# A planned order for the first token block, and the low words' three bits on ScalarE

## The chip, the cores and the metric

The kernel runs on one core of one Trainium2 chip. The metric is the device time of one execution, in microseconds (us). Before the change three runs gave 1130.69, 1131.46 and 1132.25 us, so the median is 1131.46 us.

## The reference

Three stages follow each other. The first is a decayed linear attention: for each of 4 batches and 8 heads a 64 x 64 state is carried over 768 positions. The other two are dense layers on the 3072 x 512 result, each with a width of 2048 inside. All inputs have float32 or float64 values; the two layers' weights are float64.

```python
state = gamma * state + outer(k[t], v[t])          # attention, per batch and head
y[t]  = scale * (q[t] @ state)
h = x @ w_in;  g = h * sigmoid(1.702 * h);  x = g @ w_out          # layer 1
h = x @ w_in2; g = P(h) / (Q(h) + 1e-6);    out = g @ w_out2       # layer 2, P cubic, Q quadratic in |h|
```

## The kernel before

**Tiling.** The 3072 tokens are 24 chunks of 128 (six chunks per batch). Layer 1 works on six blocks of 512 tokens, four chunks each, so chunks 0 to 3 must be through the attention before the first block can start. A block has 16 steps j, one for each 128 of the 2048 inner columns. A step has two products on TensorE: `g1(j)` (12 matmuls of 128x512 into a PSUM bank `hp`) and, two steps later, `g2(j)` (12 matmuls of 128x512 that add into four banks `o`). Between them lie a sigmoid on ScalarE (L1044), a multiply on VectorE (L1045) and the split of the result into a high part `gh` (ScalarE, L1053) and a low part `gl` (VectorE, L1054). High and low parts are fp32r, and three products of them stand for one fp32 product. While block b runs, the attention of the chunks of block b+1 is slotted between its steps.

**The chunks.** A chunk is scaled (VectorE, L715 for chunks 0 to 3, then q on VectorE at L717 and k on ScalarE at L709), transposed (PE L738, copied by ScalarE L740), scored and summed (PE L777, L800), masked and added to the state (VectorE L785, L815), and multiplied out in two halves (PE L838). The first half needs one small copy (`xh`, ScalarE L889) before the second may start; then three more copies (L882) and four subtractions (`xl`, VectorE L884) follow.

**The weights.** Layer 1's weights are 32 pieces u of 128x512, taken in the order i0, i1, i2, o0, i3, o1, i4, o2, ... (i: a piece of `w_in`, for `g1`; o: of `w_out`, for `g2`). Each piece arrives as pairs of 32-bit words of float64 values and is turned into fp32 during the first block, as its steps need it:

- `w_first`: absolute value of the high words, times 2^16 (ScalarE L523);
- `w_bits`: clamp (VectorE L529), the top three bits of the low words as an integer 0 to 7 (VectorE L530), shift and or of both (VectorE L533);
- `w_sign`: the sign (VectorE L540). The first four o pieces are kept whole in the tiles `held` here, and `g2` uses them as plain fp32 (L956);
- `w_high`, `w_low`: fp32r high part (ScalarE L554) and the rest (VectorE L562).

The tiles of some pieces are reused for later ones, so the load of a later piece waits for `w_low` of an earlier one.

**What sets the order.** All four engines and the DMA queue of SyncE (SP) work strictly in the order written. The opening (chunks 0 to 3 and the first pieces) is written by hand in `opening()`; `keep_warm(n)` puts n matmuls on zeros there. After it `prep` takes one piece per half step in a software pipeline, the main loop calls `g1` two steps ahead of `g2`, and the chunks 4 to 7 come at fixed half steps. A scheduler in the framework then settles how these streams lie beside each other. Layer 2 has a planner of its own, which the change leaves alone.

Of the kernel before, what the change touches and what calls it, by code (L numbers as in the profile page):

```python
# [23 lines left out]
KD = DM // P  # L24
KF = DFF // P
EPS = 1e-6
MAXF = float(np.array(0x4FEFFFFF, np.uint32).view(np.float32))


# [411 lines left out]
def tile_kernel(ctx: ExitStack, tc: tile.TileContext, q, k, v, w1i, w1o, w2i, w2o, pa, pb, cst, out):  # L441
# [62 lines left out]
    def w_load(layer, u):  # L504
# [11 lines left out]
            nc.sync.dma_start(out=s.rearrange("p f t -> p (f t)"), in_=src.bitcast(I32)[fc * P : (fc + 1) * P, :])  # L516
        STG[u] = s

    def w_first(u):
        s = STG[u]  # L520
        m = io.tile([P, DM], F32, tag="u", name=f"u{u}")
        U[u] = m
        nc.scalar.activation(out=m, in_=s[:, :, 1].bitcast(F32), func=ACTF.Abs, scale=2.0**16)  # L523

    def w_bits(u):
        s, m = STG[u], U[u]
        mi = m.bitcast(I32)
        lo_word = s[:, :, 0]
        nc.vector.tensor_scalar(out=m, in0=m, scalar1=2.0, scalar2=MAXF, op0=ALU.max, op1=ALU.min)  # L529
        low = nc.vector.tensor_scalar(out=lo_word, in0=lo_word.bitcast(U32), scalar1=2.0**-29, scalar2=7.0, op0=ALU.mult, op1=ALU.min)  # L530
        if PIN:
            tc.keep_in_program_order(low)
        nc.vector.scalar_tensor_tensor(out=mi, in0=mi, scalar=3, in1=s[:, :, 0], op0=ALU.logical_shift_left, op1=ALU.bitwise_or)  # L533

    def w_sign(u, in_place=True):
        s, mi = STG[u], U.pop(u).bitcast(I32)
        r = s[:, :, 1] if in_place else mi
        if in_place and u in LATER:
            r = HELD[LATER.index(u)]
        nc.vector.scalar_tensor_tensor(out=r, in0=s[:, :, 1], scalar=-(2**31), in1=mi, op0=ALU.bitwise_and, op1=ALU.bitwise_or)  # L540
        STG[u] = r.bitcast(F32)

    def w_high(layer, u, whole=True):
        nm, fc = unit(layer, u)
        if whole and layer == 1 and u in LATER:
            return
        m = STG[u]
        shape = [P, KD, P] if nm == "i" else [P, DM]
        if nm == "i":
            m = m.rearrange("p (c f) -> p c f", c=KD)  # L550
        pair = wp.tile([P, 2, *shape[1:]], F32R, tag=f"w{u}", name=f"w{nm}{layer}_{fc}")
        STG[u] = m
        W[layer, nm, fc] = (pair[:, 0], pair[:, 1])
        high = nc.scalar.copy(out=pair[:, 0], in_=m)  # L554
        if not whole:
            tc.keep_in_program_order(high)

    def w_low(layer, u, whole=True):
        if whole and layer == 1 and u in LATER:
            return  # L560
        hi, lo = W[layer, *unit(layer, u)]
        low = nc.vector.tensor_tensor(out=lo, in0=STG.pop(u), in1=hi.bitcast(F32), op=ALU.subtract)  # L562
        if not whole:
            tc.keep_in_program_order(low)
# [128 lines left out]
    def load_chunk(c):  # L693
        for nm in "qkv":
            load_raw(c, nm)
# [47 lines left out]
    def att_T(c, tg, alt=None):  # L743
        for n, nm in enumerate("qk"):
            att_T1(c, nm, tg[n], alt)
# [73 lines left out]
    def att_S(c, tg, alt=None, sums=True):  # L819
        pss = [ps(tg[n], f"pS{n}_{c}").rearrange("a x t -> a (x t)") for n in range(2)]  # L820
        scores(c, pss, 0, 0)
        if sums:
            state_sums(c, pss, {(x, n) for x in range(2) for n in range(2)})
        masks(c, pss, 0, 0, alt)
        if sums:
            states_of(c, pss)

    def att_Y0(c, tg, xh, xl, o, joint=False):

# [39 lines left out]

        def bank(n, x):
            return py[n ^ x][:, 128 * x : 128 * x + 128].rearrange("a (k t) -> a k t", t=D)

        def rest():
            half(1)
# [21 lines left out]
    def att_Y1(c):  # L898
        REST.pop(c)()
# [209 lines left out]
        chunk += n  # L1109

    NU = 2 * KF
    prepped = [0]

    after_split = {}
    tenant = {}
# [9 lines left out]
        if t:  # L1125
            tenant[t] = u

    def prep(upto):

        while prepped[0] < min(upto, NU + 2):  # L1130
            s = prepped[0]
            if 2 <= s:
                w_high(1, s - 2)
            if s < NU:
                w_first(s)
            if 1 <= s <= NU:
                w_bits(s - 1)
            if 2 <= s:
                w_low(1, s - 2)
                for u in after_split.get(s - 2, ()):  # L1140
                    w_load(1, u)
            if 1 <= s <= NU:
                w_sign(s - 1)
            prepped[0] += 1

    E = mybir.EngineType
    with tc.manual_schedule(engines={E.SP}):
        nc.vector.memset(warm, 0.0)
# [5 lines left out]
            load_raw(1, nm)  # L1154
        for nm in "qk":
            load_raw(2, nm, ch, "z")
        w_load(1, 0)
        load_raw(2, "v", ch, "z")
        both = ws.tile([P, 2, H, D], F32, tag="s", name="raw3")
        load_raw(3, "q", at=both[:, 0])  # L1160
        load_raw(3, "k", at=both[:, 1])
        load_raw(3, "v", gp, "gl")
        for u in early[1:5]:
            w_load(1, u)
# [11 lines left out]
        for nm, t in (("q", "xh"), ("k", "xl")):  # L1176
            FIRST[nm] = x_pair(t, 1, F32, f"first_{nm}")

        def T(c):
            att_T(c, ("a", "a"), "gh" if c % 2 else None)  # L1180

        def S(c):
            att_S(c, ("o2", "o1") if c % 2 else ("o0", "o1"), "gl" if c % 2 else None)

        def Y(c):
            att_Y0(c, ("h", "h"), *X0, c * P)
            keep_warm(2)
            att_Y1(c)

        def opening():  # L1190
            keep_warm(10)
            scale_chunk(0)
            att_T1(0, "q", "a")
            keep_warm(2)
            att_T1(0, "k", "a")
            scale_chunk(1)
            keep_warm(2)
            S(0)
            att_T1(1, "q", "a", "gh")
            att_T1(1, "k", "a", "gh")  # L1200
            Y(0)
            load_chunk(4)
            S(1)
            scale_chunk(2)
            keep_warm(2)
            Y(1)
            for u in early[5:9]:
                w_load(1, u)
            load_chunk(5)
            for u in early[9:]:  # L1210
                w_load(1, u)
            T(2)
            w_first(0)
            scale_chunk(3)
            keep_warm(2)
            S(2)
            w_bits(0)
            w_sign(0)
            T(3)
            w_first(1)  # L1220
            w_high(1, 0)
            Y(2)
            S(3)
            w_low(1, 0)
            for u in after_split.get(0, ()):
                w_load(1, u)
            w_bits(1)
            keep_warm(4)
            Y(3)
            w_sign(1)  # L1230
            w_first(2)
            prepped[0] = 3
            prep(4)
            keep_warm(3)
            scale_chunk(4)

        with tc.manual_schedule(engines={E.PE, E.DVE, E.Activation, E.Pool}):
            opening()
        PIN.append(True)
        for x in range(2):  # L1240
            held = ws.tile([P, 2, DM], I32, tag="s", name=f"held{x}")
            HELD += [held[:, 0], held[:, 1]]
        nxt = 0
        conv0 = KF + 2
        XS0 = 4 * KF + KF - 2
        XB = []
# [27 lines left out]
                        if f:  # L1274
                            f()

        for i in range(-lead[1], NS):
            p0 = 2 * i + 6
            prep(p0)
            while nxt < NS and nxt - lead[steps[nxt][0]] <= i:  # L1280
                j = nxt
                nxt += 1
                g1(j)
                act1_a(j)
                prep(p0 + 1)
                act1_b(j)
            if i == -1:
                scale_chunk(5)
            if 0 <= i - KF + 2 < WHOLE:
                w_high(1, LATER[i - KF + 2], False)  # L1290
                w_low(1, LATER[i - KF + 2], False)
            if i == KF:
                tc.keep_in_program_order(nc.scalar.activation(out=ab[:, 6:7], in_=ab[:, 5:6], func=ACTF.Abs))
            if i < 0:
                continue
            for f in todo[i][0]:
                f()
            g2(i)
            layer, bi, fc, t0, n = steps[i]
            if fc == KF - 1 and bi < 5:  # L1300
                evac(bi)
            for f in todo[i][1]:
                f()

            if i >= XS0:
                x_piece(i)
            if i >= NS - 4:
                load_wo(2 * (i - NS + 4))
                load_wo(2 * (i - NS + 4) + 1)
# [46 lines left out]
```

## Time and profile before

| | |
|---|---|
| median of 3 runs | 1131.46 us (1130.69 to 1132.25) |
| the profiled execution: its own time, its span | 1132.12 us, 1130.3 us |
| TensorE, matmuls | busy 1108.3 us (98%), 7489 matmuls |
| VectorE (DVE) | busy 878.7 us (78%), 1293 instructions |
| ScalarE (ACT) | busy 637.7 us (56%), 962 instructions |
| mean granted TensorE clock | 0.994 of full speed |

The span is the time from the first to the last instruction; 1.8 us of the profiled execution's time lie outside it. Busy time of TensorE is not useful time: matmuls overlap each other at their ends, and the warm-up matmuls on zeros count too. Where work per step matters, read the distance from one start to the next, not the durations: a VectorE instruction shown with 0.69 us is followed by the next one 0.60 us later.

### The profile page before, as it was taken

What the parts mean: (1) busy time and instruction counts of PE and PEld (TensorE: products, weight loads), DVE (VectorE), ACT (ScalarE), POOL (GpSimd) and SP (SyncE); (2) the same over time, 40 slices, a digit from 0 to 9 for tenths busy, and PEclk for the clock granted to TensorE, in tenths of its full rate; (3) what the DMA queues carried; (4) which work ended last, traced back from release to release, by engine and by line L of the source; (5) the groups of instructions that cost most, each with busy time, mean ns of one, the idle gap of its engine ahead of it and who ended that gap; (6) DMA issues with size and microseconds to landing.
All of it is one profiled execution on the core that took longest, in us unless ns stands there. A gap on an engine that the chain in (4) does not pass through costs nothing.

```text
span 1130.3 us, 19172 instructions
## 1 busy us (share of the span) xinstructions
PE 1108.3 (98%) x7489; PEld 894.4 (79%) x7489; DVE 878.7 (78%) x1293; ACT 637.7 (56%) x962; POOL 31.8 (3%) x52
## 2 busy tenths in 40 slices
PE   7899999999999999999999999999999999999998
PEld 4567788788888888888888778887888888888887
DVE  5799966757676556677477789899988899988895
ACT  3456533333333323334345677887887787787882
POOL 0000000001010000011000000000000000000000
PEclk9899999999999999999999999999999999999999
DMA  9954255677576576865588985841454822454001
GB/s 224 321 161 113 71 126 142 159 196 219 146 172 202 137 181 178 208 194 178 204 301 283 375 260 189 292 172 46 123 157 130 309 91 76 120 159 124 25 38 38
DMA packets 235353, 193.30 MB, mean 171 GB/s; under 512 B 150784, under 2 KB 183936, under 8 KB 235264
## 3 DMA queue, kind: packets, MB, share of 16 engines
q1 hardware_dynamic: 228864, 169.01, 51.5%
q0 software_dynamic: 6400, 23.07, 5.6%
q8 instruction: 59, 0.97, 0.4%
q14 instruction: 30, 0.25, 0.1%
HBM read 134.37 MB, written 57.67 MB: 170 GB/s over the span
## 4 chain that ended last, share of the span: by engine, by line
PE 78%; DVE 12%; DMA 4%; ACT 3%; issue 2%; SPq 1%; DVEq 0%; ACTq 0%
PE o L246 20%; PE hp L937 17%; PE a L148 11%; PE o L958 6%; PE o L959 6%; PE o L960 6%; PE c L148 6%; PE b L148 3%; PE pY L838 2%; DVE u L533 1%; DVE s L540 1%; DMA rawk<-in_k_dram 1%; PE pY L800 1%; DMA xc<-xo 1%; DMA s<-in_moe_w_in_dram 1%
## 5 line engine op out<-in xcount | busy, mean ns | idle before, releaser
L937 PE MATMUL hp<-xh,wi 128*128 128x512 f32 x768 | 256.7, 396 | 4.1 <-DVE wi L562 3.2
L937 PEld LDWEIGHTS hp<-xh,wi 128*128 128x128 f32 x768 | 144.8, 189 | 37.1 <-DVE wi L562 3.9
L937 PE MATMUL hp<-xl,wi 128*128 128x512 f32 x384 | 149.9, 392 | 0.0
L148 PE MATMUL a<-x,wi 128*128 128x512 f32 x576 | 145.5, 390 | 1.9 <-DMA wi<-wc 1.8
L958 PE MATMUL o<-gh,wo 128*128 128x512 f32 x368 | 146.3, 398 | 0.4 <-DVE wo L562 0.4
L1045 DVE TENSOR_TENSOR z<-hp,z 128x512 f32<-128x512 f32 x96 | 65.9, 686 | 102.5 <-ACT z L1044 102.3
L1044 ACT ACTIVATE z<-hp 128x512 f32<-128x512 f32 x96 | 57.2, 596 | 155.2 <-PE hp L937 143.0
L959 PE MATMUL o<-gl,wo 128*128 128x512 f32 x368 | 143.8, 391 | 0.2 <-DVE gl L1054 0.2
L960 PE MATMUL o<-gh,wo 128*128 128x512 f32 x368 | 143.6, 390 | 0.0
L148 PEld LDWEIGHTS a<-x,wi 128*128 128x128 f32 x576 | 107.9, 188 | 25.4 <-DVE z L313 1.9
L1053 ACT CAST gh<-z 128x512 fp32r<-128x512 f32 x92 | 57.1, 621 | 67.1 <-DVE z L1045 67.0
L308 DVE SCALAR_TENSOR_TENSOR z<-z,ab,w 128x1024 f32<-128x1024 f32 x48 | 61.5, 1280 | 31.3 <-ACT w L306 31.2
L937 PEld LDWEIGHTS hp<-xl,wi 128*128 128x128 f32 x384 | 72.5, 189 | 15.2 <-issue 0.5
L1054 DVE TENSOR_TENSOR gl<-z,gh 128x512 fp32r<-128x512 f32 x92 | 63.2, 687 | 26.9 <-ACT gh L1053 25.7
L958 PEld LDWEIGHTS o<-gh,wo 128*128 128x128 f32 x368 | 69.0, 188 | 16.7 <-DVE wo L562 1.1
L960 PEld LDWEIGHTS o<-gh,wo 128*128 128x128 f32 x368 | 69.1, 188 | 14.5
L959 PEld LDWEIGHTS o<-gl,wo 128*128 128x128 f32 x368 | 69.1, 188 | 14.3 <-DVE gl L1054 0.5
L322 ACT ACTIVATE gh<-h 128x1024 fp32r<-128x1024 f32 x48 | 50.9, 1059 | 41.7 <-PE o L246 36.8
L148 PE MATMUL c<-x,wi 128*128 128x512 f32 x288 | 73.3, 390 | 0.4 <-DMA wi<-wc 0.4
L148 PEld LDWEIGHTS c<-x,wi 128*128 128x128 f32 x288 | 53.9, 188 | 12.1 <-ACT xo L349 0.8
L311 DVE TENSOR_TENSOR p<-h,p 128x1024 f32<-128x1024 f32 x48 | 58.5, 1219 | 5.5 <-ACT p L307 5.5
L312 DVE SCALAR_TENSOR_TENSOR p<-p,ab,h 128x1024 f32<-128x1024 f32 x48 | 61.4, 1279 | 0.5
(208 smaller groups left out, 2050.4 us busy)
## 6 DMA issues: line engine op xcount, KB each, us to landing
wi<-wc SPq DMA_DIRECT2D x168, 256.0 KB, 2.8
s<-in_moe_w_in_dram SPq DMA_DIRECT2D x32, 512.0 KB, 6.4
s<-in_moe_w_out_dram SPq DMA_DIRECT2D x32, 512.0 KB, 5.5
x<-xc SPq DMA_DIRECT2D x28, 512.0 KB, 8.4
wc<-s POOLq DMA_DIRECT2D x24, 512.0 KB, 4.4
xc<-xo SPq DMA_DIRECT2D x36, 256.0 KB, 2.9
rawv<-in_v_dram SPq DMA_DIRECT2D x24, 256.0 KB, 4.3
rawq<-in_q_dram SPq DMA_DIRECT2D x40, 128.0 KB, 5.3
```

Of the source, the lines that this page charges most:

```text
L148: nc.tensor.matmul(bank, wt[:, a, k], XT[s, x, k][:, b], start=begin and y == 0, stop=y == 5, skip_group_check=True)
L246: nc.tensor.matmul(ACC[d], a[:, x, r], w[:, b], start=g == 0 and x == 0 and y == 0, stop=g == NG - 1 and x == 1 and y == 2)
L308: dve("q", [("ab", m)], lambda: stt(out=v["z"], in0=v["z"], scalar=ab[:, 6:7], in1=v["w"], op0=ALU.mult, op1=ALU.add))
L311: dve("p1", [("id", m)], lambda: nc.vector.tensor_tensor(out=v["p"], in0=h, in1=v["p"], op=ALU.mult))
L312: dve("p2", [("p1", m)], lambda: stt(out=v["p"], in0=v["p"], scalar=ab[:, 1:2], in1=h, op0=ALU.add, op1=ALU.mult))
L937: nc.tensor.matmul(hp, w[:, kk, :], t[kk // 2][:, kk % 2, :], start=(x == 0), stop=(x == len(terms) - 1))
L958: nc.tensor.matmul(o, wl[:, r], gh, start=a, stop=False)
L959: nc.tensor.matmul(o, wh[:, r], gl, start=False, stop=False)
L960: nc.tensor.matmul(o, wh[:, r], gh, start=False, stop=z)
L1044: nc.scalar.activation(out=z, in_=hp, func=ACTF.Sigmoid, scale=1.702)
L1045: nc.vector.tensor_tensor(out=z, in0=hp, in1=z, op=ALU.mult)
L1054: nc.vector.tensor_tensor(out=gl, in0=z, in1=gh.bitcast(F32), op=ALU.subtract)
```

## The change

The three bits of a layer 1 piece's low words are made by ScalarE (`w_low_act`, one `Copy` activation with the scale 7.49 / 2^32, read as unsigned, written as int32) for all 32 pieces; VectorE's L530 stays for layer 2's weights alone. `opening()`, `prep` and the first block's part of the main loop are replaced by `first_block()`: it lists every piece of work from the first transposes to step 13's `g2` (and `g1` up to step 15) with its engine, an assumed duration, a due time, what it needs and which buffers it takes, and then places one after another: of the work that could start within 0.05 us of the earliest, the one with the earliest due time. SyncE's loads are placed in the same way. `keep_warm` matmuls go in only where that plan has a gap on TensorE, 21 in all where there were 33. The tiles `held` are taken when the first of them is written. From step 14 on each engine's order is the one of before, but for some instructions near the seam.

```diff
+    def w_low_act(u):
+        lo_word = STG[u][:, :, 0]
+        nc.scalar.activation(out=lo_word, in_=lo_word.bitcast(U32), func=ACTF.Copy, scale=LOW_SCALE)
...
-    def w_bits(u):
+    def w_bits(u, low_word=True):
         s, m = STG[u], U[u]
         mi = m.bitcast(I32)
         lo_word = s[:, :, 0]
         nc.vector.tensor_scalar(out=m, in0=m, scalar1=2.0, scalar2=MAXF, op0=ALU.max, op1=ALU.min)
-        low = nc.vector.tensor_scalar(out=lo_word, in0=lo_word.bitcast(U32), scalar1=2.0**-29, scalar2=7.0, op0=ALU.mult, op1=ALU.min)
-        if PIN:
-            tc.keep_in_program_order(low)
+        if low_word:
+            low = nc.vector.tensor_scalar(out=lo_word, in0=lo_word.bitcast(U32), scalar1=2.0**-29, scalar2=7.0, op0=ALU.mult, op1=ALU.min)
+            if PIN:
+                tc.keep_in_program_order(low)
         nc.vector.scalar_tensor_tensor(out=mi, in0=mi, scalar=3, in1=s[:, :, 0], op0=ALU.logical_shift_left, op1=ALU.bitwise_or)
...
         for nm in "qk":
             load_raw(2, nm, ch, "z")
-        w_load(1, 0)
         load_raw(2, "v", ch, "z")
         both = ws.tile([P, 2, H, D], F32, tag="s", name="raw3")
         load_raw(3, "q", at=both[:, 0])
         load_raw(3, "k", at=both[:, 1])
+        w_load(1, 0)
         load_raw(3, "v", gp, "gl")
...
+            def D_(j):
+                return 29.0 + 6.3 * j
...
+                op("ACT", ("first", u), 0.57, due, [("ld", u)], lambda u=u: w_first(u), [("u", [("sign", u)])])
+                bits = [("first", u)]
+                on_act = u in LOW_ON_ACT
+                if on_act:
+                    op("ACT", ("word", u), 0.57, due, [("first", u)], lambda u=u: w_low_act(u))
+                    bits = [("word", u)]
+                op("DVE", ("bits", u), 0.94 if on_act else 1.28, due, bits, lambda u=u, on_act=on_act: w_bits(u, not on_act))
...
-            S(2)
-            w_bits(0)
-            w_sign(0)
-            T(3)
-            w_first(1)
-            w_high(1, 0)
-            Y(2)
-            S(3)
-            w_low(1, 0)
...
+                early_ = min(can)[0]
+                t, rank, n = min((x for x in can if x[0] <= early_ + 0.05), key=lambda x: x[1])
+                eng, dur, rank, deps, fn, takes = left.pop(n)
...
+                    elif gap > 0.5:
+                        keep_warm(1 if gap < 1.0 else 2)
...
-        for i in range(-lead[1], NS):
-            p0 = 2 * i + 6
-            prep(p0)
+        for i in range(FIRST_STEPS, NS):
```

The first place is ScalarE in the opening, from the first work on piece 0 (its tile is `s_0`, piece 1's is `s_1`) to the last copies `xh` of chunk 2 (`pY_2`). Before:

```order
L523 ACTIVATE u_517<-s_0_211 128x512
L740 COPY qT_575<-pTq_570 128x512
L740 COPY kT_582<-pTk_577 128x512
L523 ACTIVATE u_584<-s_1_220 128x512
L554 CAST wi_0_586<-s_0_211 128x512
L889 CAST xh_0_233<-pY_2_588 128x2x64
L882 CAST xh_0_233<-pY_2_589 128x2x64
L882 CAST xh_1_234<-pY_2_589 128x2x64
L882 CAST xh_1_234<-pY_2_588 128x2x64
```

In the changed kernel:

```order
L528 ACTIVATE u_524<-s_0_216 128x512
L1262 COPY kT_548<-pTk_519 128x512
L522 ACTIVATE s_0_216<-s_0_216 128x512
L899 CAST xh_0_233<-pY_2_530 128x2x64
L891 CAST xh_0_233<-pY_2_531 128x2x64
L891 CAST xh_1_234<-pY_2_531 128x2x64
L891 CAST xh_1_234<-pY_2_530 128x2x64
L528 ACTIVATE u_639<-s_1_220 128x512
L522 ACTIVATE s_1_220<-s_1_220 128x512
L899 CAST xh_0_233<-pY_3_621 128x2x64
L564 CAST wi_0_674<-s_0_216 128x512
L891 CAST xh_0_233<-pY_3_622 128x2x64
```

The cast of piece 0 (`wi_0`) stood ahead of all four copies of chunk 2; it now stands behind the first copy of chunk 3 and ahead of its last three. Two new activations on low words stand among them.

The second place is VectorE around steps 4 to 6, where pieces 10 to 15 are made (`wi_6` is piece 10, `wo_4` 11, `wi_7` 12, `wo_5` 13). Before:

```order
L529 TENSOR_SCALAR u_1073<-u_1073 128x512
L530 TENSOR_SCALAR s_12_491<-s_12_491 128x512
L562 TENSOR_TENSOR wo_4_1102<-s_11_489,wo_4_1102 128x512
L533 SCALAR_TENSOR_TENSOR u_1073<-u_1073,s_12_491 128x512
L540 SCALAR_TENSOR_TENSOR s_12_491<-s_12_491,u_1073 128x512
L1054 TENSOR_TENSOR gl_1081<-z_1068,gh_1080 128x512
L529 TENSOR_SCALAR u_1104<-u_1104 128x512
L530 TENSOR_SCALAR s_13_493<-s_13_493 128x512
L562 TENSOR_TENSOR wi_7_1127<-s_12_491,wi_7_1127 128x512
L533 SCALAR_TENSOR_TENSOR u_1104<-u_1104,s_13_493 128x512
```

In the changed kernel:

```order
L572 TENSOR_TENSOR wi_6_1080<-s_10_738,wi_6_1080 128x512
L550 SCALAR_TENSOR_TENSOR s_13_761<-s_13_761,u_1045 128x512
L1353 TENSOR_TENSOR gl_1097<-z_1068,gh_1096 128x512
L534 TENSOR_SCALAR u_1089<-u_1089 128x512
L539 SCALAR_TENSOR_TENSOR u_1089<-u_1089,s_12_764 128x512
L572 TENSOR_TENSOR wo_5_1101<-s_13_761,wo_5_1101 128x512
L550 SCALAR_TENSOR_TENSOR s_12_764<-s_12_764,u_1089 128x512
L534 TENSOR_SCALAR u_1123<-u_1123 128x512
L539 SCALAR_TENSOR_TENSOR u_1123<-u_1123,s_15_768 128x512
L572 TENSOR_TENSOR wi_7_1144<-s_12_764,wi_7_1144 128x512
L550 SCALAR_TENSOR_TENSOR s_15_768<-s_15_768,u_1123 128x512
```

L530's instructions on `s_12` and `s_13` are gone from VectorE, and each piece's clamp and or (L529 and L533, now L534 and L539) stand next to each other; the order of clamp, or, sign and rest over the pieces is otherwise alike.

## Rows read from the trace of the kernel before

**Rows 1.** Windows: us, busy (instructions) per engine, TensorE clock, DMA share, GB/s.
```profile
0.00:34.50 34.50, 26.42 (x562) 16.52 (x562) 19.36 (x59) 11.57 (x30) 0.20 (x4) 0.90 1.00 233
34.50:60.00 25.50, 22.49 (x198) 15.58 (x199) 19.57 (x41) 13.83 (x36) 0.00 (x0) 0.93 1.05 340
60.00:100.00 40.00, 40.00 (x326) 29.51 (x325) 39.50 (x82) 26.12 (x58) 0.00 (x0) 1.00 0.42 114
100.00:145.76 45.76, 43.60 (x346) 33.98 (x345) 45.20 (x95) 23.98 (x47) 0.00 (x0) 1.00 0.45 104
145.76:1130.30 984.54, 975.80 (x6061) 798.82 (x6059) 755.05 (x1021) 562.19 (x793) 31.60 (x48) 1.00 0.56 170
```

**Rows 2.** Timeline of TensorE, marks of the first block: start, us, idle before.
```profile
34.50 2.09 PE L937 MATMUL hp<-xh,wi 128*128 128x512 f32 x8 [0.81 <-DVE xl L884]
...
47.70 0.50 PE L937 MATMUL hp<-xh,wi 128*128 128x512 f32 x1 [2.29 <-DVE wi L562]
...
73.75 0.79 PE L937 MATMUL hp<-xh,wi 128*128 128x512 f32 x1
...
131.43 0.50 PE L937 MATMUL hp<-xh,wi 128*128 128x512 f32 x1 [0.77 <-DVE wi L562]
...
145.76 0.39 PE L958 MATMUL o<-gh,wo 128*128 128x512 f32 x1
```

**Rows 3.** Timeline of the opening, where chunk 2 waits.
```profile
23.32 0.69 DVE L540 SCALAR_TENSOR_TENSOR s<-s,u 128x512 int32<-128x512 int32 x1
24.05 0.65 ACT L554 CAST wi<-s 128x512 fp32r<-128x512 f32 x1 [1.46 <-DVE s L540]
...
24.91 0.70 PE L838 MATMUL pY<-qT,st 64*64 64x64 f32 x16 [2.42 <-ACT xh L889]
```

**Rows 4.** Windows of the opening, columns as in rows 1.
```profile
26.00:28.00 2.00, 1.53 (x54) 1.34 (x46) 0.88 (x4) 0.60 (x3) 0.00 (x0) 0.50 0.64 132
28.00:30.00 2.00, 1.70 (x17) 0.95 (x18) 0.98 (x3) 0.00 (x0) 0.00 (x0) 0.50 0.78 176
```

**Rows 5.** Timeline of VectorE, a piece in the full stretch.
```profile
72.41 0.42 DVE L529 TENSOR_SCALAR u<-u 128x512 f32<-128x512 f32 x1
72.74 0.42 DVE L530 TENSOR_SCALAR s<-s 128x512 int32<-128x512 uint32 x1
73.08 0.68 DVE L562 TENSOR_TENSOR wo<-s,wo 128x512 fp32r<-128x512 f32 x1
```

**Rows 6.** Chain of waits: start, us, what.
```profile
154.09 2.72 PE hp L937 x12
```

**Rows 7.** Timeline of TensorE, parts of a step and of a chunk.
```profile
70.71 3.60 PE L956 MATMUL o<-z,held 128*128 128x512 f32 x8
...
76.97 0.69 PE L777 MATMUL pS<-qT,kT 64*64 64x64 f32 x32
...
78.05 0.50 PE L958 MATMUL o<-gh,wo 128*128 128x512 f32 x1
...
81.00 0.46 PE L838 MATMUL pY<-qT,st 64*64 64x64 f32 x16
...
81.63 0.50 PE L937 MATMUL hp<-xh,wi 128*128 128x512 f32 x1
...
93.50 0.60 PE L738 MATMUL pTq<-cs,rawq 128*128 128x128 f32 x4
...
94.29 0.48 PE L937 MATMUL hp<-xh,wi 128*128 128x512 f32 x1
```

**Rows 8.** Timeline of ScalarE: a piece's activation, and keys scaled in eight parts.
```profile
36.33 2.03 ACT L709 ACTIVATE rawk<-rawk,cs 128x64 f32<-128x64 f32 x8
...
74.99 0.68 ACT L523 ACTIVATE u<-s 128x512 f32<-128x512 f32 x1
75.56 0.67 ACT L554 CAST wi<-s 128x512 fp32r<-128x512 f32 x1
```

**Rows 9.** Windows, of line L530 on VectorE alone: us, busy (count), clock, DMA share, GB/s.
```profile
34.50:145.76 111.26, 12.62 (x30) 0.98 0.57 162
```

More of the change, by code (lines that the diff above doesn't have):

```diff
@@ L26 @@
 EPS = 1e-6
+LOW_SCALE = 7.49 / 2.0**32
 MAXF = float(np.array(0x4FEFFFFF, np.uint32).view(np.float32))
@@ L538, in w_sign @@
         if in_place and u in LATER:
+            if not HELD:
+                for x in range(2):
+                    held = ws.tile([P, 2, DM], I32, tag="s", name=f"held{x}")
+                    HELD.extend([held[:, 0], held[:, 1]])
             r = HELD[LATER.index(u)]
@@ L826, in att_S, with att_Y0 @@
             states_of(c, pss)
-    def att_Y0(c, tg, xh, xl, o, joint=False):
+    def att_Y0(c, tg, xh, xl, o, joint=False, pieces=None):
         vr, sm, qT = RAW[c, "v"], SM[c], QK[c, "q"]
@@ L873, in bank, with clear, outs, lows @@
             return py[n ^ x][:, 128 * x : 128 * x + 128].rearrange("a (k t) -> a k t", t=D)
+        def clear():
+            del RAW[c, "v"], SM[c], QK[c, "q"], ST[c, "mid"]
+            ST.pop(c, None)
+        def outs():
+            for n, x in ((0, 1), (1, 0), (1, 1)):
+                nc.scalar.copy(out=part(xh, n, x), in_=bank(n, x))
+        def lows():
+            for n, x in ((0, 0), (0, 1), (1, 0), (1, 1)):
+                nc.vector.tensor_tensor(out=part(xl, n, x), in0=bank(n, x), in1=part(xh, n, x).bitcast(F32), op=ALU.subtract)
+        if pieces is not None:
+            half(0)
+            pieces[c] = (lambda: nc.scalar.copy(out=part(xh, 0, 0), in_=bank(0, 0)), lambda: (half(1), clear()), outs, lows)
+            return
         def rest():
@@ L1111, in tile_kernel @@
     NU = 2 * KF
-    prepped = [0]
     after_split = {}
@@ L1126, in tile_kernel @@
             tenant[t] = u
[L1128 to L1144, printed above, removed]
     E = mybir.EngineType
@@ L1177, in tile_kernel @@
             FIRST[nm] = x_pair(t, 1, F32, f"first_{nm}")
[L1179 to L1190, printed above, removed]
-            keep_warm(10)
[L1192 to L1215, printed above, removed]
-            S(2)
-            w_bits(0)
-            w_sign(0)
-            T(3)
-            w_first(1)
-            w_high(1, 0)
-            Y(2)
-            S(3)
-            w_low(1, 0)
[L1225 to L1235, printed above, removed]
@@ L1237, in tile_kernel @@
         with tc.manual_schedule(engines={E.PE, E.DVE, E.Activation, E.Pool}):
-            opening()
+            first_block()
         PIN.append(True)
[L1240 to L1243, printed above, removed]
+        nxt = FIRST_STEPS + 2
         conv0 = KF + 2
@@ L1284, in tile_kernel @@
                 act1_a(j)
-                prep(p0 + 1)
                 act1_b(j)
-            if i == -1:
-                scale_chunk(5)
             if 0 <= i - KF + 2 < WHOLE:
@@ L1293, in tile_kernel @@
                 tc.keep_in_program_order(nc.scalar.activation(out=ab[:, 6:7], in_=ab[:, 5:6], func=ACTF.Abs))
-            if i < 0:
-                continue
             for f in todo[i][0]:
```

181 lines of the change are left out of this document (added).

## The prediction

> **What bounds the kernel now.** I read the windows by stage first, then TensorE's marks in the timeline, then what stands behind its waits. Up to the last mark, 145.76 us, TensorE has done `g1(0)` to `g1(16)`, `g2(0)` to `g2(13)` and chunks 0 to 7; the next matmul is the first of `g2(14)` [rows 2]. From there to the end 984.54 us go by, in which TensorE is busy for 975.80 us [rows 1]. In them each engine's order stays as it was, so a `g2(14)` that starts earlier moves the end by the same amount. The change can win or lose time in two stretches only: the opening, 0 to 34.50 us, and the first block, 34.50 to 145.76 us, which is 111.26 us long [rows 2].
>
> In the first block VectorE sets the pace. It is busy for 39.50 of 40 us and then for 45.20 of 45.76 us, while ScalarE is busy for 26.12 and 23.98 us of these [rows 1]. TensorE looks just as full from 60 to 100 us, but its durations overlap and stretch; the distances show the truth. From `g1(6)` at 73.75 us to `g1(14)` at 131.43 us eight steps take 57.68 us, 7.21 us a step, and what TensorE waits for at 47.70 and 131.43 us is VectorE's last instruction on a weight piece [rows 2]. A `g1` or `g2` fed in time takes 2.72 us [rows 6].
>
> In the opening the order itself costs time. ScalarE's cast of piece 0 waits for VectorE's sign, ends at 24.70 us, and only then comes the copy that chunk 2 needs, so TensorE stands for 2.42 us [rows 3]. Its granted clock is 0.50 (1.2 GHz) from 26 to 30 us, after that idle time [rows 4].
>
> **The change part by part.** The sum is made against the profiled execution, 1132.12 us (span 1130.3 us and 1.8 us around it), 0.66 us above the median of the three runs.
>
> *VectorE loses L530.* One takes 0.34 us from its start to the next (72.74 to 73.08 us) [rows 5]. 30 of them lie in the first block [rows 9], so 10.2 us go. VectorE's busy time there, 19.57 + 39.50 + 45.20 = 104.3 us [rows 1], falls to 94.1 us.
>
> *ScalarE gains one activation per piece.* The trace has none that reads integers. Bounds by the nearest rows: not less than VectorE's 0.34 us [rows 5]; not more than the 2.03 us that a tile of the same size takes in eight parts [rows 8]. Nearest is the activation on the other words of the same tile, 74.99 to 75.56 us, 0.57 us [rows 8]; I take that. 30 x 0.57 = 17.1 us on top of 13.83 + 26.12 + 23.98 = 63.9 us [rows 1] make 81.0 us. That hides as long as the block lasts longer; the cover is gone above (111.3 - 63.9) / 30 = 1.58 us per activation. The wait it adds is VectorE's clamp and or behind it; behind that on VectorE stand other pieces' instructions, so a piece is later by a few tenths and is made earlier in the order.
>
> *What is late next.* TensorE's own work in the first block: 17 `g1` and 10 `g2` at 2.72 us are 73.4 us [rows 6]; 4 `g2` on whole fp32 weights at 3.04 us (70.71 to 73.75 us), each with a `g1` behind it that takes 3.22 instead of 2.72 us (73.75 to 76.97 us), are 14.2 us; a chunk takes 0.79 us for transposes (93.50 to 94.29), 1.08 us for scores and sums (76.97 to 78.05) and twice 0.63 us for its halves (81.00 to 81.63), for 4 chunks 12.5 us [rows 2, 7]. That makes 100.1 us, more than VectorE's 94.1 us: TensorE is the next bound. Two engines so close can't both be fed without loss. VectorE lost 111.3 - 104.3 = 7.0 us to waits in this stretch; for TensorE I take 2.6 us. So the first block takes 102.7 us, 8.6 us less. The ends: 100.1 us, and 111.3 us where waits take the place of L530.
>
> *The opening's order.* The cast of piece 0 now stands behind chunk 3's first copy, so the 2.42 us at 24.91 us [rows 3] go. In the 4 us at the low clock TensorE was busy for 1.53 + 1.70 = 3.2 us [rows 4], which at 2.4 GHz would take 1.6. For the finer mesh of chunks and fewer warm-up matmuls I take 1.0 us, between 0 and 3. The sum is 5.0 us: the first `hp` matmul at 29.5 instead of 34.50 us. The ends are 0 and 7.0 us.
>
> *SP's queue.* Piece 0's load moves behind chunk 2's values and chunk 3's queries and keys; chunk 5's loads and pieces 5 and 7 go ahead of piece 6. The DMA share is 1.05 from 34.5 to 60 us and 0.42 after [rows 1]: the queue runs far ahead of the steps, so I cost the moves in the block at nothing. Without that cover, a late piece holds ScalarE, behind which all copies of the chunks stand. Piece 0 is such a place, since `w_first(0)` stands ahead of chunk 3's key copy; that is a rival below. `held` and the later loads wait for the same pieces as before.
>
> Sum: 1132.12 - 5.0 - 8.6 = 1118.5 us; less the 0.66 us, 1117.9 us.
>
> **A rule that speaks against it.** The rows show VectorE full and ScalarE at 26.12 of 40 us [rows 1], and 0.57 against 0.34 us for one operation on a piece's words [rows 5, 8]. The Trainium skill ("ScalarE: Activation LUTs", Rules for kernel authors) says to use VectorE, not ScalarE, for multiplications and minima. The trace agrees about the single operation; if the dearer one counted, the block would grow by 30 x 0.23 = 6.9 us, which needs a ScalarE that is the full engine (rival 4). The same page (What ACT_TABLE_LOAD costs) gives 186 ns and 0.833 ns per element, with 93 ns of overlap; an estimate from it is 0.52 us, by which ScalarE would come to 79.5 us.
>
> **The rivals.**
>
> 1. *Only the block gains.* Piece 0 lands late, ScalarE waits on it ahead of chunk 3's copies, or the clock falls with 21 warm-ups instead of 33; the first `hp` matmul stays at 34.5 us. For it: that wait has just this form in rows 3. Against it: piece 0 is needed no earlier than before. 1132.12 - 8.6 - 0.66 = 1122.9 us.
> 2. *Only the opening gains.* Engines wait for each other in turn, and the step keeps its 7.21 us. For it: four strict queues that are 79 to 97% full. Against it: VectorE's 94.1 us and its freedom to make pieces ahead. 1126.5 us.
> 3. *Both go to their ends.* Opening 7.0 us less, block 100.7 us: 1132.12 - 7.0 - 10.6 - 0.66 = 1113.9 us.
> 4. *Slower: ScalarE becomes the bound.* If an activation from unsigned to signed integers costs the upper bound, ScalarE has 63.9 + 30 x 2.03 = 124.8 us to do in the first block, 13.5 us more than the block lasts now; with 5.0 us won in the opening the kernel takes 8.5 us more, 1140.0 us. It decides from (111.3 + 5.0 - 63.9) / 30 = 1.75 us per activation on. Against it: strided words cost ScalarE 0.57 us in rows 8.
> 5. *It doesn't do what it says.* The planned order meets other loads than assumed and gives back all it wins: 1131.5 us.
>
> **How the numbers follow.** Chances: forecast 0.56, rival 1 0.17, rival 2 0.09, rival 3 0.10, rival 4 0.05, rival 5 0.03. The forecast's own range is 1114.5 to 1121.5 us (opening 3.5 to 6.5 us, block 100.7 to 104.7 us). A range of 1113.5 to 1125.0 us takes in the forecast, rivals 1 and 3, which is 0.83 of the chance, and leaves out the far ends: the slow activation and a block without gain. About 0.2% (2.3 us) can be told from no change. The forecast and rivals 1 to 3 are faster by more, 0.92; rival 5 is the same, 0.03; rival 4 is slower, 0.05.
>
> **What would show it.** Right: no L530 in the first 130 us; 32 new activations at about 0.57 us from start to start; the first `hp` matmul near 29.5 us; `g2(14)` near 132 us; VectorE below 95% busy in the block, TensorE's waits on `wi` under 1 us in sum; 984.5 us from `g2(14)` to the end, unchanged. Rival 1 shows a first `hp` matmul after 33 us, rival 2 a step of over 7 us, rival 4 an activation over 1.5 us with ScalarE full. The prediction is wrong at its root if the time after `g2(14)` changes by over 2 us.

## The result and the profile after

The changed kernel takes 1120.61 us (median of five runs, 1119.06 to 1121.83); the kernel before, run beside it, 1131.95 us (1130.69 to 1132.67). The ratio is 0.9904, with a 95% interval of 0.989 to 0.9918: 1% faster, by some 11 us. The profiled execution of the change took 1119.06 us, the fastest of the five; its span is 1117.3 us.

The windows by stage come first, cut at TensorE's marks as in [rows 1], with the same columns (us, busy and instructions of PE, PEld, DVE, ACT, POOL, then TensorE's clock, DMA share, GB/s):

```profile
0.00:30.34 30.34, 24.44 (x549) 16.17 (x549) 17.96 (x52) 11.96 (x30) 0.20 (x4) 0.86 0.99 216
30.34:60.00 29.66, 29.66 (x230) 19.98 (x228) 27.08 (x55) 25.19 (x58) 0.00 (x0) 0.97 1.07 346
60.00:100.00 40.00, 40.00 (x377) 30.76 (x376) 38.54 (x77) 33.98 (x75) 0.00 (x0) 1.00 0.61 158
100.00:134.30 34.30, 34.30 (x266) 27.54 (x265) 32.12 (x60) 21.61 (x40) 0.00 (x0) 1.00 0.38 85
134.30:1117.30 983.00, 974.31 (x6061) 797.68 (x6059) 754.81 (x1020) 562.78 (x794) 31.39 (x48) 1.00 0.56 170
```

The opening is 30.34 us long instead of 34.50, the first block 103.96 instead of 111.26, and the rest 983.00 instead of 984.54 us [rows 1]. VectorE is busy for 27.08 + 38.54 + 32.12 = 97.7 of the block's 103.96 us (94%), ScalarE for 80.8 us (78%). The two marks themselves, in the timeline of TensorE, answer to [rows 2]:

```profile
30.34 3.04 PE L964 MATMUL hp<-xh,wi 128*128 128x512 f32 x8
...
134.30 0.39 PE L985 MATMUL o<-gh,wo 128*128 128x512 f32 x1
```

Here is all that TensorE waited for up to 30.4 us, longest in total first (us, times, longest). From 30.4 to 134.4 us the same view is empty: the waits of 2.29 and 0.77 us on VectorE's weight pieces [rows 2] are gone and none has come in their place.

```profile
PE pTk L1258 <- DVE xl L895: 1.3, 1, 1.3
PE wt L1181 <- DVE ab L1175: 1.2, 1, 1.2
PE pS L787 <- ACT kT L1262: 1.2, 2, 0.9
PE pY L848 <- issue: 0.8, 1, 0.8
PE pTq L1258 <- DVE first_q L725: 0.6, 1, 0.6
PE pTk L1258 <- DVE first_k L725: 0.5, 2, 0.3
```

The new activation on the low words, first as the group of its line (count, shortest, median and longest duration in ns), then in the timeline of ScalarE. From its start to the next instruction's it takes 0.64 us at 71.48 us; in the opening 0.57 (21.92 to 22.49 us) and 0.59 (27.39 to 27.98 us):

```profile
L522 ACT ACTIVATE s<-s x32: 649/675/697, 21.9 to 129.1; 128x512 int32<-128x512 uint32 x32
```

```profile
70.90 0.67 ACT L528 ACTIVATE u<-s 128x512 f32<-128x512 f32 x1
71.48 0.67 ACT L522 ACTIVATE s<-s 128x512 int32<-128x512 uint32 x1
72.12 0.60 ACT L891 CAST xh<-pY 128x128 fp32r<-128x128 f32 x3
```

### The profile page after: what moved, and what is told of

The parts are those of the page before. It is cut to its first block, busy times and chain, and to the rows that moved or that the text cites. A ratio compares the mean times of both kernels' runs of the same rounds, so it can differ in the third digit from the quotient of the medians.

```text
span 1117.3 us, 19179 instructions
## 1 busy us (share of the span) xinstructions
PE 1102.7 (99%) x7477; PEld 892.1 (80%) x7477; DVE 870.5 (78%) x1261; ACT 655.5 (59%) x994; POOL 31.6 (3%) x52
## 4 chain that ended last, share of the span: by engine, by line
PE 86%; DVE 5%; DMA 4%; SPq 2%; ACT 2%; issue 1%; DVEq 0%; ACTq 0%
PE hp L964 20%; PE o L247 20%; PE a L149 11%; PE o L985 7%; PE o L986 6%; PE o L987 6%; PE c L149 6%; PE b L149 3%; PE pY L848 2%; DMA xs<-x 1%; PE o L983 1%; SPq L696 1%; DMA s<-in_moe_w_in_dram 1%; PE pY L810 1%; DMA xc<-xo 1%
## 5 line engine op out<-in xcount | busy, mean ns | idle before, releaser
L1071 ACT ACTIVATE z<-hp 128x512 f32<-128x512 f32 x80 | 47.7, 596 | 149.8 <-PE hp L964 139.5
L1072 DVE TENSOR_TENSOR z<-hp,z 128x512 f32<-128x512 f32 x80 | 54.9, 687 | 101.9 <-ACT z L1071 98.6
L1080 ACT CAST gh<-z 128x512 fp32r<-128x512 f32 x80 | 49.6, 621 | 59.9 <-DVE z L1072 59.8
L1081 DVE TENSOR_TENSOR gl<-z,gh 128x512 fp32r<-128x512 f32 x80 | 55.0, 688 | 25.8 <-ACT gh L1080 24.9
L310 ACT ACTIVATE w<-z,ab 128x1024 f32<-128x1024 f32 x48 | 55.0, 1150 | 12.7 <-DVE z L309 12.7
```

The lines of the kernel that those rows point to most:

```text
L310: act("rs", [("q", m)], lambda: A(out=v["w"], in_=v["z"], func=ACTF.Abs_reciprocal_sqrt, bias=ab[:, 7:8]))
L1072: nc.vector.tensor_tensor(out=z, in0=hp, in1=z, op=ALU.mult)
L1081: nc.vector.tensor_tensor(out=gl, in0=z, in1=gh.bitcast(F32), op=ALU.subtract)
```

## The experiments

**The order alone.** All words stay on VectorE, in the planned order. The plan is made anew, with VectorE's longer time for a piece, so the engines' orders aren't those of the change in all places.

```diff
-        LOW_ON_ACT = set(range(NU))
+        LOW_ON_ACT = set()
```

> The planned order as in the change, but the low words' bits on VectorE for all 32 pieces, as before the change. Theory A (VectorE's load per piece sets the first block's pace): VectorE has 104 us of work in the block again, so the block takes 107 to 110 us instead of 104.0; the first hp matmul stays at about 30 us; the time is 1123.5 to 1127 us. Theory B (the planned order alone brings the gain, the move of the bits nothing): block about 104 us, time 1119.5 to 1121.5 us.

Measured: 1129.64 us (1124.95 to 1130.64), ratio 0.998 (0.9968 to 0.9992). The first `hp` matmul comes at 29.45 us, so the opening's gain is there, and steps 0 to 10 keep the change's pace. Then it is given back: `g1(13)` starts 10.3 us after `g1(12)`, and `g2(14)` at 145.23 us, where before it was 145.76 [rows 2]. Theory A's direction was right and its size wrong: the block took 115.8 us, not 107 to 110. TensorE's two longest waits in the block (us, times, longest):

```profile
PE hp L964 <- DVE wi L572: 4.5, 2, 3.1
PE o L985 <- DVE wo L572: 0.7, 2, 0.6
```

**The move alone.** The order of before, with the words on ScalarE behind each piece's absolute value.

```diff
+            low = nc.scalar.activation(out=lo_word, in_=lo_word.bitcast(U32), func=ACTF.Copy, scale=LOW_SCALE)
...
-        low = nc.vector.tensor_scalar(out=lo_word, in0=lo_word.bitcast(U32), scalar1=2.0**-29, scalar2=7.0, op0=ALU.mult, op1=ALU.min)
```

> The old order with the low words' bits on ScalarE, right behind each piece's first activation, for layer 1 alone. Theory A: the first hp matmul stays at 34 to 35 us, the block falls from 111.3 to 104 to 107 us, and the time is 1125 to 1128 us. Theory B: block 110 to 112 us, time 1131 to 1133 us.

Measured: 1131.59 us (1129.08 to 1135.32), ratio 1.0008 (0.9994 to 1.0021): nothing, and theory A's time is missed. VectorE has room now and can't use it. In the timeline of ScalarE the copy of chunk 4 waits for TensorE for 7.95 us, and the activations of the next pieces are queued behind it:

```profile
46.19 0.57 ACT L747 COPY kT<-pTk 128x512 f32<-128x512 f32 x1
54.71 0.27 ACT L896 CAST xh<-pY 128x128 fp32r<-128x128 f32 x1 [7.95 <-PE pY L845]
54.87 0.68 ACT L524 ACTIVATE u<-s 128x512 f32<-128x512 f32 x1
55.44 0.69 ACT L527 ACTIVATE s<-s 128x512 int32<-128x512 uint32 x1
```

**More work on ScalarE.** The change, with each piece's absolute value computed twice.

```diff
-        nc.scalar.activation(out=m, in_=s[:, :, 1].bitcast(F32), func=ACTF.Abs, scale=2.0**16)
+        for _ in range(1 if PIN else 2):
+            nc.scalar.activation(out=m, in_=s[:, :, 1].bitcast(F32), func=ACTF.Abs, scale=2.0**16)
```

> The change with each piece's first activation (absolute value, 0.57 us) done twice on ScalarE, in the same order: 30 x 0.57 = 17 us more work for ScalarE in the block. Theory A (TensorE is the bound now, ScalarE is covered): ScalarE rises to about 97% of the block and costs 0 to 4 us, 1120.5 to 1124.5 us. Rival C (ScalarE's queue is as good as full already, what is added comes through): 15 us or more, 1135 us or above.

Measured: 1125.24 us (1123.38 to 1126.67), ratio 0.995 (0.9932 to 0.9968), 3.7 us more than the change run beside it, for some 17 us of added work. Rival C falls: ScalarE isn't what bounds the change. But its cover is used up here; the window of its busiest stretch (columns as above) shows it busy for 39.00 of 40 us:

```profile
60.00:100.00 40.00, 39.15 (x371) 29.76 (x370) 37.11 (x73) 39.00 (x84) 0.00 (x0) 1.00 0.56 142
```

**The change once more,** beside these three.

> The change as it is, run beside the others for comparison on the same chip: 1119 to 1122 us.

Measured: 1121.58 us (1118.16 to 1123.09), ratio 0.9914 (0.9895 to 0.9933). In its profiled execution the first `hp` matmul came at 33.61 us and `g2(14)` at 137.7: the block again took 104.1 us, but the opening 3.3 us more than in the first profile.

**The opening: three trials.** The plan assumes that piece 0 lands at 19.3 us; ScalarE waited for it until 20.89. One kernel tells the plan the true time, one adds eight warm-up matmuls, one does both.

```diff
-            for u, t in zip(early[:5], (19.3, 22.8, 24.3, 25.7, 27.2)):
+            for u, t in zip(early[:5], (20.9, 22.8, 24.3, 25.7, 27.2)):
```

```diff
+        MORE = {("T", 3, "k"): 5, ("scores", 3): 3}
...
+                    if n in MORE:
+                        keep_warm(MORE[n])
```

> The change with the plan told that piece 0 lands at 20.9 us, as the trace of the change shows, not at 19.3: ScalarE then makes the copies of chunk 3's transposes and the first of chunk 2 before it touches piece 0. Theory D (ScalarE's wait for piece 0 holds the chunks, TensorE stands and its clock falls from 22 to 32 us): first hp matmul 1 to 2 us earlier than in a run of the change beside it, time 1119 to 1120.5 us. Rival E (the loads and the chain of chunk 3 set the opening, this wait only comes in front of another): within 0.7 us of the change, 1120.9 to 1122.2 us.

> The change with 8 more matmuls on zeros in the two gaps in which TensorE stands before its clock falls: 5 ahead of the transposes of chunk 3's keys, 3 ahead of chunk 3's scores. Theory D: the clock stays at 2.4 GHz up to the first hp matmul, the 6 us of chunk work done at half speed take 3 us, the first hp matmul comes 2 to 3.5 us earlier, time 1117.5 to 1119.5 us. Rival E: the clock stays up but TensorE waits for the same loads and copies, time 1120.5 to 1122.5 us.

> Both of these. Theory D: 3 to 4.5 us less than the change, 1116.5 to 1118.5 us. Rival E: 1120 to 1122 us.

Measured: 1120.94 (ratio 0.9912, 0.9898 to 0.9926), 1119.19 (0.9904, 0.989 to 0.9918) and 1121.74 us (0.992, 0.9908 to 0.9933). None can be told from the change. The first and the third lie in rival E's range, so theory D isn't borne out there; the second lies in D's range, and its clock did stay at full speed up to 28 us, but its interval is the change's, so D stays open for it. The first `hp` matmul came at 31.57, 30.76 and 30.10 us, between the 30.34 and 33.61 us of the change's own two profiles. What all three show is another stop of TensorE, which waits for nothing but "issue": 4.2 us in the first, 2.4 and 1.0 in the second, 1.9 and 0.9 in the third.

**More work on VectorE.** The change, with the clamp (0.42 us long, 0.34 us to the next start) done twice on each piece.

```diff
-        nc.vector.tensor_scalar(out=m, in0=m, scalar1=2.0, scalar2=MAXF, op0=ALU.max, op1=ALU.min)
+        for _ in range(2 if not low_word else 1):
+            nc.vector.tensor_scalar(out=m, in0=m, scalar1=2.0, scalar2=MAXF, op0=ALU.max, op1=ALU.min)
```

> The change with each layer 1 piece's clamp (0.34 us) done twice on VectorE, in the same order; ScalarE does all it does in the change. Theory A2 (with the planned order VectorE's total work decides, counted from the opening on, and the words' 0.34 us per piece were the whole difference between this order with and without them on VectorE): steps 0 to 10 come as in the change, the loss shows in steps 11 to 14, time 1128 to 1131 us. Rival F (the words on ScalarE matter by what they do to the order there, not by VectorE's load): 1121 to 1124 us.

Measured: 1134.15 us (1132.33 to 1136.13), ratio 1.0032 (1.0021 to 1.0044): about 13 us slower than the change, and slower than before. Rival F falls: VectorE's work isn't hidden. Theory A2 has the direction, but 1128 to 1131 us is missed, and the loss begins in steps 3 to 8 already, earlier than expected (in step 3 TensorE also stands 1.7 us for nothing but "issue"). Much of the miss lies in the edit: the second clamp reads what the first has just written and starts 0.45 us after it (median of 32 pairs, all 0.44 to 0.46), so it costs more than 0.34 us. TensorE's longest wait in the block (us, times, longest), and the timeline of VectorE at such a pair:

```profile
PE o L987 <- DVE gl L1354: 7.0, 7, 1.6
```

```profile
60.61 0.88 DVE L535 TENSOR_SCALAR u<-u 128x512 f32<-128x512 f32 x2
```

**Can the old order be mended?** Two repairs of the move alone: chunks 4 to 7 three half steps later, and each piece made a step further ahead.

```diff
+            if bi == 1:
+                at_pos = [min(p + 3, 2 * room) for p in at_pos]
```

```diff
-            p0 = 2 * i + 6
+            p0 = 2 * i + 8
```

> The order of before with the words on ScalarE, and the pieces of chunks 4 to 7 placed three half steps later in the first block. With the words alone ScalarE stood 7.95 us at 46.8 us for chunk 4's first copy, with the activations of the next weight pieces behind it, and VectorE was busy for only 19.6 of the 30 us from 30 to 60. Theory G, that this one hold kept VectorE from using the room that the move had given it: the pieces of steps 2 to 4 are made before the copy, VectorE is busy for over 24 of these 30 us, g2(14) starts at 138 to 143 us and the kernel takes 1123 to 1128 us. Theory H, that the old order holds an engine in turn wherever a chunk stands between its steps: the hold turns up later, at another copy, and the time stays within 2.5 us of 1131.5 us.

> The order of before with the words on ScalarE, and each weight piece made one step (two pieces) further ahead; chunks 4 to 7 stay at their half steps. Theory G' , that only the distance between a piece and its step was too small once ScalarE is held by a copy: VectorE can fall behind for a step without TensorE seeing it, its waits on wi and wo fall from 2.7 us to under 1 us, and the kernel takes 1123 to 1128 us. Theory H, that the hold on ScalarE is what sets the pace: the pieces ahead stand behind the same copies, the tiles of the pieces are not free any earlier, and the time stays within 2.5 us of 1131.5 us.

Measured: 1132.77 us (ratio 1.0018, 1.0006 to 1.003) and 1129.85 us (0.9993, 0.9981 to 1.0004). Both times are theory H's; G and G' fall. In the first, ScalarE is free of chunk 4's copy, and VectorE stands instead, for chunk 4's scores, which have moved up ahead of the weight pieces; ScalarE then stands for VectorE. Timelines of VectorE and ScalarE:

```profile
53.44 0.75 DVE L792 TENSOR_TENSOR sm<-pS,cs 128x256 f32<-128x256 f32 x2 [5.79 <-PE pS L807]
...
54.90 0.68 DVE L547 SCALAR_TENSOR_TENSOR held<-s,u 128x512 int32<-128x512 int32 x1
```

```profile
47.10 0.61 ACT L747 COPY kT<-pTk 128x512 f32<-128x512 f32 x1
55.62 0.68 ACT L524 ACTIVATE u<-s 128x512 f32<-128x512 f32 x1 [7.91 <-DVE held L547]
```

In the second, TensorE's wait on `wi` did fall from 2.7 to 0.8 us, as G' said, but a wait of 1.9 us on `held` and others on VectorE and ScalarE came in its place, and VectorE still stood idle for 12.9 us of the block.

**What the "issue" stop waits for.** It stands at a fixed count of matmuls. The window that ends just ahead of it, in the change, in the kernel with more warm-up matmuls, and in the kernel before, whose order is another, holds 474 matmuls each time:

```profile
0.00:25.70 25.70, 19.90 (x474) 13.61 (x475) 14.85 (x44) 9.07 (x21) 0.20 (x4) 0.93 1.04 227
```

```profile
0.00:26.70 26.70, 19.94 (x474) 12.88 (x475) 14.72 (x44) 9.20 (x21) 0.20 (x4) 1.00 1.06 233
```

```profile
0.00:28.25 28.25, 21.02 (x474) 13.77 (x474) 15.04 (x46) 10.14 (x25) 0.20 (x4) 0.94 1.01 225
```

The eight added matmuls moved the stop eight matmuls up in the work: it stood after the tenth of the 16 matmuls of chunk 2's second half, and now stands after the second. Some 2.5 us before TensorE goes on, a packet of 0.02 MB of the "instruction" queue moves (at 23.40 us in the change, where TensorE goes on at 25.80). Two kernels hold SyncE's loads back for a while, by a 64-byte store that has to wait for a copy on ScalarE: of chunk 3's queries in the one, of its keys in the other.

```diff
-        for u in early[1:5]:
-            w_load(1, u)
+        w_load(1, early[1])
+        gate = dr.tile([1, 16], F32, name="gate")
...
                         nc.scalar.copy(out=t, in_=PT.pop((c, nm)))
+                        if (c, nm) == (3, "k"):
+                            nc.sync.dma_start(out=gate, in_=(t[0:1, 0, 0:16] if len(t.shape) == 3 else t[0:1, 0:16]))
+                            for u in early[2:5]:
+                                w_load(1, u)
```

> The changed kernel; on SyncE a 64-byte store that reads chunk 3's transposed queries (ready at about 19.0 us) stands ahead of the loads of pieces 2, 3 and 4 and of all that follow, so the queue issues nothing between about 18 and 19 us. In every trace of the planned order TensorE stops without a wait after the same matmul, its 474th, for 0.8 to 4.2 us at 22 to 26 us, while the DMA share is 1.0; a 16 KB instruction packet moves some 2 us before it goes on. Theory J, that TensorE waits there for its next instructions, which stand behind the loads in the DMA rings: a small gap helps a little, the stall is still there after the 474th matmul, 0.5 to 3 us, and the time is 1118.5 to 1121 us. Rival K, that the stall doesn't depend on the loads: 1120 to 1122 us, the stall as long as before.

> The same with the store reading chunk 3's transposed keys (ready at about 22.0 us), so that no load is issued from about 18 to 22 us and the DMA rings run dry by about 23 us. Theory J (TensorE's next instructions stand behind the loads): the stall after the 474th matmul falls under 0.5 us, the first hp matmul comes at 27.5 to 29.5 us and, as pieces 2 to 4 and chunk 4 come in time all the same, the time is 1116.5 to 1119.5 us. Rival K (the stall doesn't depend on the loads): the stall stays at 0.8 to 4.2 us, 1120 to 1122 us. Rival L (the loads were needed early): the stall goes, but ScalarE waits for piece 2 or chunk 4 after 30 us and gives it back, 1120 to 1125 us.

Measured: 1121.29 us (ratio 0.9922, 0.9907 to 0.9937) and 1119.0 us (0.9903, 0.9888 to 0.9917). In both, TensorE starts chunk 3's key transposes, its 349th matmul and the next three, at about the same time (22.03 and 21.62 us). With the early gate loads fill the DMA engines again (share about 1.0) when the instruction packet comes; it moves at 26.57 us, 4.5 us after the 349th matmul, and TensorE stands after its 474th matmul until 29.08. The DMA view of 26 to 27 us, and TensorE's timeline:

```profile
q1 hardware_dynamic: 425, 0.35, 105.6%
q8 instruction: 1, 0.02, 7.0%
```

```profile
26.09 0.66 PE L848 MATMUL pY<-sm,rawv 64*64 64x64 f32 x10
29.08 0.49 PE L848 MATMUL pY<-sm,rawv 64*64 64x64 f32 x6 [2.33 <-issue]
```

With the late gate the DMA share falls to 0.03, the packet moves at 23.26 us, 1.6 us after the 349th matmul, with nothing beside it, and the stop is gone; TensorE reaches its 475th matmul at 25.65 us, 2.4 us after the packet, so it only just fits. Counted from the kernel's start the packet is hardly earlier than in the change, where it moves at 23.40 us among loads; but there the 349th matmul had started at 19.90 us, 3.5 us before. The DMA view of 23 to 24 us, TensorE's timeline, and the windows around it:

```profile
DMA packets 1, 0.02 MB, mean 16 GB/s; under 512 B 0, under 2 KB 0, under 8 KB 0
```

```profile
25.40 0.59 PE L848 MATMUL pY<-sm,rawv 64*64 64x64 f32 x16
25.92 0.39 PE L1181 MATMUL wt<-warm 128*128 128x512 bf16 x1
...
29.24 2.12 PE L964 MATMUL hp<-xh,wi 128*128 128x512 f32 x8
```

```profile
22.00:24.00 2.00, 2.00 (x58) 1.67 (x60) 0.14 (x1) 1.32 (x3) 0.00 (x0) 0.50 0.03 8
24.00:26.00 2.00, 2.00 (x86) 1.93 (x78) 1.17 (x3) 0.00 (x0) 0.00 (x0) 0.70 0.49 133
26.00:28.00 2.00, 1.50 (x39) 0.71 (x39) 1.97 (x8) 1.88 (x6) 0.00 (x0) 1.00 1.07 396
```

Counted from the 349th matmul, the packet moves after 1.6 us here and after 2.8 to 5.1 us in the nine other traces of the planned order. So this one trace bears out theory J for the stop, and K falls. For the kernel's time it settles less: the late gate's interval overlaps the change's, its TensorE waits 1.2 us for chunk 4's queries later on (a little of rival L), and its block took 104.9 us. It isn't shown to beat the change. Neither gate touches the wait ahead of the 349th matmul, 3.2 us in both, which the view of waits puts down to VectorE's clamp of piece 0 (L534). It is likely a stop of the same kind, as the section on the prediction says of the change's second profile.

## Why the prediction was right

The forecast was 1117.9 us, the median is 1120.61; in the profiled execution 1118.5 stood against 1119.06 us. The end came by the way that the sum described, with two terms too large. That the profiled execution ends within 0.6 us of its sum is in part luck: the opening and the block together gained 2.1 us less than forecast, and the rest, which the change leaves alone, happened to be 1.5 us shorter; it was also the fastest of the five.

- **The opening, -5.0 us forecast, -4.2 measured** in the first profile, -0.9 in the second (33.61 us). The 2.42 us for chunk 2's copy [rows 3] went, as said. What I called "the finer mesh of chunks" left out two things: ScalarE's wait for piece 0, which the plan expected earlier, and the "issue" stop, which was there before as well (0.77 us) and lasts 0.8 to 3.2 us in the two profiles of the change. In the first, behind the idle time ahead of 22 us, the granted clock is 0.50 (1.2 GHz) up to the first `hp` matmuls, as in [rows 4]. Timeline of ScalarE and TensorE, and windows, of the change:

```profile
20.89 0.66 ACT L528 ACTIVATE u<-s 128x512 f32<-128x512 f32 x1 [1.92 <-DMA s<-in_moe_w_in_dram]
```

```profile
19.90 0.63 PE L1258 MATMUL pTk<-cs,first_k 128*128 128x128 f32 x4 [1.32 <-DVE xl L895]
...
22.08 1.20 PE L787 MATMUL pS<-qT,kT 64*64 64x64 f32 x31 [0.93 <-ACT kT L1262]
...
25.80 0.49 PE L848 MATMUL pY<-sm,rawv 64*64 64x64 f32 x6 [0.82 <-issue]
```

```profile
22.00:24.00 2.00, 1.92 (x70) 1.92 (x74) 0.71 (x2) 0.74 (x3) 0.00 (x0) 0.50 1.00 284
...
30.00:32.00 2.00, 2.00 (x6) 1.31 (x5) 1.52 (x6) 1.73 (x5) 0.00 (x0) 0.50 1.02 282
```

  The second profile has rival 1's sign, a first `hp` matmul after 33 us, and about its price: that execution took 1122.77 us, rival 1 stood at 1122.9. Its cause was another. ScalarE waited only 0.85 us for piece 0; TensorE stood 3.16 us after its 474th matmul and, ahead of the 349th, longer than in the first profile:

```profile
21.76 0.76 PE L1258 MATMUL pTk<-cs,first_k 128*128 128x128 f32 x4 [2.70 <-DVE u L534]
```

  The clamp named there (L534) can't be what it waited for: it reads what ScalarE's activation on piece 0 writes, and in the first profile of the same kernel these transposes started at 19.90 us, before that activation at 20.89. An instruction packet moved at 19.12 us, 2.64 us before TensorE went on, so this is likely the same kind of stop; no run settles it.

- **The first block, 102.7 us forecast, 103.96 measured** (104.1 and 104.9 in two other profiles). That TensorE would be the next bound was right in so far as it no longer waits in the block. The 2.6 us that I added for waits had no row behind it, and no wait came; TensorE's own work was the larger. My 100.1 us took 2.72 us for every product on split weights [rows 6]; in the chain of waits (start, us, what) most of those that stand behind a chunk's short matmuls take more, and `g1(0)`, which starts at the low clock, takes 3.8 us:

```profile
50.33 2.99 PE hp L964 x12
...
92.03 2.95 PE hp L964 x12
...
117.94 2.72 PE hp L964 x12
```

- **VectorE, 94.1 us forecast, 97.7 measured.** The block's instructions on the low words are gone, but 1.4 us of other work no longer fits in the shorter opening, and in a looser row, in which fewer instructions overlap the one before, the others count in full. That VectorE would no longer bind was wrong. The table has the two stretches, opening and block, for six profiles; the lines under it are the blocks of the four that aren't shown elsewhere (columns as above):

| profile | opening, us | VectorE busy in it, us | block, us | VectorE busy in it, us | VectorE idle in it, us |
|---|---|---|---|---|---|
| before | 34.50 | 19.36 | 111.26 | 104.27 | 7.0 |
| old order, words moved | 34.68 | 18.70 | 112.47 | 97.53 | 14.9 |
| planned order, words on VectorE | 29.45 | 17.55 | 115.78 | 109.46 | 6.3 |
| the change | 30.34 | 17.96 | 103.96 | 97.74 | 6.2 |
| the change, second profile | 33.61 | 17.80 | 104.09 | 97.82 | 6.3 |
| the change, clamp twice | 32.03 | 18.36 | 116.37 | 110.61 | 5.8 |

```profile
34.68:147.15 112.47, 106.98 (x869) 80.50 (x869) 97.53 (x188) 79.64 (x170) 0.00 (x0) 0.97 0.57 161
29.45:145.23 115.78, 109.62 (x967) 81.35 (x966) 109.46 (x224) 65.19 (x142) 0.00 (x0) 0.98 0.59 167
33.61:137.70 104.09, 104.09 (x870) 78.42 (x869) 97.82 (x189) 80.79 (x171) 0.00 (x0) 0.99 0.62 175
32.03:148.40 116.37, 107.14 (x871) 78.00 (x869) 110.61 (x220) 80.92 (x171) 0.00 (x0) 0.99 0.57 157
```

  In the planned order VectorE's idle time in the block is 5.8 to 6.6 us in nine profiles of ten, whatever its work (9.7 us in the one with more work on ScalarE), and the block's length follows VectorE's work one for one: 11.7 us more work than in the change make it 11.8 us longer, 12.9 more make it 12.4 longer. In the change TensorE shows no wait either, so there both engines are at their limit.
- **The two gains are not a sum.** The step that didn't hold is the independence of the terms, by which rival 2 was priced: "only the opening gains" at 1126.5 us. The order alone, with an opening 5.05 us shorter, took 1129.64; in its profile the block is 4.5 us longer than before. VectorE has 5.2 us more to do in it: 1.8 us that the longer opening of before still held, and 3.4 us by which the same work takes longer. This plan puts the low words' instruction directly ahead of the one that reads its result; 29 such pairs are 0.46 us apart, where L530 is followed by work on another piece after 0.34 us [rows 5]. So the order alone was tried with a handicap, and no run shows what it is worth without. The move alone takes the work away, but in the old order an engine stands in turn for a chunk's instruction placed ahead of its input (14.9 us idle). Done apart, the move gives nothing and the order 0.2%; together 1%. The forecast held because both parts were in.
- **ScalarE's activation, 0.57 us forecast, 0.57 to 0.64 measured,** with ScalarE at 78% in the block. Rival 4 needed 1.75 us. The Trainium skill ("ScalarE: Activation LUTs", Rules for kernel authors) prefers VectorE for such work; here the slower engine was the better place, since VectorE's time counts in full and ScalarE's in part (17 us more of it cost 3.7). By the Trainium skill ("ScalarE: Activation LUTs", What ACT_TABLE_LOAD costs) the estimate was 0.52 us, a little under the trace.
- **The rest, unchanged forecast, -1.5 us measured:** 983.0 us in the first profile of the change, 983.3 in the second, 981.6 to 986.2 in the other kernels, which leave it alone too. That is the spread of single executions.
- **SyncE's moves** cost nothing in the block: the view of waits from the first `hp` matmul to `g2(14)` has no load for TensorE, VectorE or ScalarE. Piece 0, the place I named as uncovered, was late by 1.92 us on ScalarE; with the plan corrected the time stayed the same.

## What to carry to other kernels

Before adding up two gains on engines that feed each other, ask what each would be worth without the other: room on an engine was worth nothing here while a strict order made another engine stand ahead of it, and a better order was worth 0.2% while the full engine had no less to do. Count the full engine's work from the kernel's start to the seam (here `g2(14)`), not per stage: a head start that doesn't shorten that sum comes back as a wait at its end. Work may go to the engine that takes longer for it if that one's time counts only in part, and doubling a cheap operation on each engine measures by how much it counts, if the doubled one's real cost is read from the trace.

## What the hardware showed that was not expected

TensorE stops without a wait after its 474th matmul, for 0.8 to 4.2 us, in 12 of the 14 traces, and an instruction packet of 0.02 MB moves 2.3 to 2.6 us before it goes on in each of them. With loads beside it (DMA share 0.8 to 1.1 from 22 to 26 us) the packet moves 2.8 to 5.1 us after TensorE's 349th matmul in the planned order; in the one trace with the DMA idle (0.03) it moves 1.6 us after it, and there is no stop. The other trace without one is the old order with the pieces further ahead: its packet moves at 26.06 us, in good time, as TensorE reaches its 475th matmul only at 29.26 us. Other stops stand after 220 matmuls (before, 1.16 us) and 348 (with more warm-up, 1.00 us); the three places are 128 and 126 matmuls apart. The trace doesn't say for which engine a packet is, and why the stop varies so much from run to run of one kernel stays open.

On VectorE an instruction that reads what the one directly ahead of it wrote starts 0.12 us later than one that doesn't: 0.46 instead of 0.34 us behind L530 in the kernel before, 0.45 us between the doubled clamps.
